# A table of due positions rewritten: stores of V times rms_g, loads, conversions and late attention placed anew in a memory attention and SwiGLU kernel

## The chip, the cores and the metric

The kernel runs on one core of one Trainium2 chip. The metric is the device time of one execution in microseconds (us). Its engines are TensorE (PE, with its weight loads shown apart as PEld), VectorE (DVE), ScalarE (ACT), GpSimd (POOL) and SyncE (SP); in this kernel SP issues every DMA, in the order of its own list. Each engine works through its list strictly in order and waits where an operand isn't there yet.

## The reference

```python
# q, k, v: (8 batches, 8 heads, 576, 64); phi: (8, 8, 576, 32); all float32
a = phi - max(phi, over the 32); a = exp(a); a = a / (sum(a) + 1e-9)
k_m = einsum('bhsm,bhsd->bhmd', a, k)          # sums over all 576 positions
v_m = einsum('bhsm,bhsd->bhmd', a, v)
scores = q @ k_m.T / sqrt(64)
attn = softmax(scores over the 32 memories)
x = (attn @ v_m), heads side by side           # 4608 tokens x 512
# then a gated network on x, with one rms_g for each of the 512 columns
xn = x / sqrt(mean(x * x) + 1e-6) * rms_g
out = (silu(xn @ w_gate) * (xn @ w_val)) @ w_out   # 512 -> 1536 -> 512, float32
```

`setup_inputs` multiplies q and k by 200, so the scores are large and the result has to be computed in full float32 accuracy.

## The kernel before, in words

**Numbers.** Every product of the gated network is made of three: each operand is split into a high and a low part (`ath`/`atl`, `xh`/`xl`, `wh`/`wl`, `oh`/`ol`, `hh`/`hl`) and high-high, high-low and low-high are added up in PSUM. The network is not applied to x itself: V times rms_g (`vg`) is multiplied into the weights first (`vp`, `vq`), so that the attention weights meet a 64-wide product `xh`/`xl` of V and W, and 1/rms is computed from a Gram matrix (`gram`) of V and the attention weights, and multiplied into these weights (L236).

**Part 1 (0 to about 150 us).** The eight batches go through one after the other, and two of them are a pair. For a batch: `load_phi` and eight loads of k and v into buffers `kv` (each is free again when the product matmuls of the batch that used it have ended); the softmax of phi, for which DVE takes maxima (`mc`, L549), PE turns them (`mt` L556, `mr` L573), DVE subtracts (L582) and ACT takes the exponential into `e_bd` (L592); 72 matmuls `kvp` (L623) that make k_m and v_m in one PSUM tile; 64x1 matmuls with ones (L638) that add the denominators into the same tile, from `e_bd` directly or from partial sums `es` that POOL has made; then on DVE `si` (L646, L647), `im` (L649), `kb` and `vb` (L655); the transposes `kvt` on PE (L667), their copies on ACT (L681), `vg` on POOL (L688), and the Gram products (L697, L706). For batches 4 to 7 `store()` (L713, and L716 for `gram`) writes `vg` and, for the second batch of a pair, the Gram matrix to DRAM; the first sweep reads both back.

The attention of pairs 0 and 1 is done here too: for each of four steps q is loaded and turned, 36 matmuls make the scores S (L763), DVE takes maxima and subtracts them (`mxs` L774, L776), ACT takes the exponential, the sums `sm` are made (by one DVE reduction, L790; or by a POOL addition that halves the row and a DVE reduction, L796; or by five POOL additions), POOL multiplies by 1/`sm` (L803, tile `a`). Then `x_steps`: PE turns `a` (`tp`, L208), DVE or ACT copies it into `at` (L218), PE multiplies by the Gram matrix (`xp`, L265/270), DVE squares and adds (L283), a chain of short DVE steps makes 1/rms (`rinv`, L294 to L311), PE spreads it (`rp`, L228), DVE multiplies it into `at` (L236), and ACT and POOL split `at` (L256, L257).

Beside this the first weights are converted: `raw` is loaded, DVE makes a rounded copy in integer arithmetic (`ex`, `mi`, L387 to L417), a multiplication (`w`, L433) on POOL or DVE closes it, and the split parts are stored to `wd`, `od` (L457, L462) for the second sweep.

**Sweeps.** The first sweep (about 150 to 560 us) takes pairs 0 and 1 against twelve blocks of weights, in 24 units: `vp` (L964), `pg` and `pv` (L1000), the gate (L1008, L1009), the split (L1027, L1028), `po` (L1047), `acc` (L1055), and the output (L1059). Spread among them are the conversion of the other weights and the late attention of pairs 2 and 3. The second sweep (units 24 to 47) takes pairs 2 and 3; for it the weight parts are reloaded from DRAM (`reload`, L475), `vq` (L914) multiplies V into them, and `send` (L945) moves the result to its place.

**What sets the order.** One dictionary, `PRM`, gives a due position to every step. The program collects pairs of position and function, sorts them by position and calls them; the lists of the engines come out of that order, after a scheduler of the framework has arranged it by its own estimate of times, which it does again for each program. So a position is a wish, and the order of the lists has to be read from the program built. Those that this text names are `K_AT` and `POST` (products and DVE steps of a batch), `PREP`, `PD` (softmax of phi), `KD` (loads of k and v), `SO`, `X_AT` (attention of pairs 0 and 1), `VD` (the stores of `vg`), `CV` (conversion), `U` and `RL` (units of the second sweep and their reloads). `XE`, `SUM`, `CE` and `ESN` don't place a step: they choose the engine of a copy L218, the way of a sum, the engine of a multiplication L433, and how many of a batch's partial sums POOL adds up ahead of L638. Of this are the lines

```python
ev.append((K_AT[b] + 6 * PRM["KP"] + PRM["POST"][5] + PRM["VD"][b - 2 * G], store))
on_pool = kind == 2 or n >= 2 or PRM["CE"][n] & (1 << kind)
for _, f in sorted(ev, key=lambda e: e[0]):
    f()
```

## Time and profile before

| what | value |
|---|---|
| median of 3 runs | 895.3 us (894.73 to 896.17) |
| profiled execution, its own time | 894.66 us |
| its span | 892.9 us, so 1.76 us lie around the span |
| TensorE clock granted, mean | 0.971 |
| PE busy | 829.4 us (93%), 5919 matmuls |
| DVE, ACT, POOL busy | 543.8, 400.7 and 326.7 us |
| DMA | 131.62 MB, 147 GB/s on average |

All durations that follow come from this one profiled execution; its time is 0.64 us under the median. In the rows, L numbers are lines of the kernel before, an arrow points from the operand to the result, and an expression in brackets at a row's end tells how long the engine had waited ahead of the instruction and for whom. "x36" at the end of a row of the timeline is the number of like instructions that the row stands for.

### The profile page before, as it was taken

Reading aid. Unit: us, or ns where it says so; the run is one execution under the profiler, and the core shown is the slowest. Engines: PE = TensorE matmul, PEld = TensorE weight load, DVE = VectorE, ACT = ScalarE, POOL = GpSimd, SP = SyncE. Lnnn points to the kernel's source line nnn. Section 1 sums busy time; section 2 is a strip of 40 time slices with the busy share of each in tenths; the row PEclk is TensorE's granted clock in tenths of the full one; section 3 lists DMA queues with packets and bytes.
Section 4 is the critical chain, followed back from the end, with each engine's and each line's share of the span. In section 5 each row is a group of like instructions: output and inputs, shape, how many; then the busy total and the mean of one; then the engine's idle time right before and its main releaser. Section 6 shows DMA issues by size and latency. Waiting matters only on the chain.

```text
span 892.9 us, 15977 instructions
## 1 busy us (share of the span) xinstructions
PE 829.4 (93%) x5919; PEld 738.3 (83%) x5919; DVE 543.8 (61%) x982; ACT 400.7 (45%) x715; POOL 326.7 (37%) x272
## 2 busy tenths in 40 slices
PE   4889576999999999998999999999999999999997
PEld 4777466989897988987997988878989898999996
DVE  5587965888757887877987746412344344444434
ACT  1666442676854664645654433335423223233220
POOL 3464744465435454354363531412212112122120
PEclk9889787999999999999999999999999999999999
DMA  8987542545335254253353455575655555553437
GB/s 277 323 276 241 204 145 85 150 145 158 108 98 143 77 146 118 78 182 118 91 145 115 147 129 114 139 216 136 171 139 130 135 144 144 140 149 87 92 93 170
DMA packets 110245, 131.62 MB, mean 147 GB/s; under 512 B 45140, under 2 KB 74840, under 8 KB 110168
## 3 DMA queue, kind: packets, MB, share of 16 engines
q1 hardware_dynamic: 110168, 130.60, 51.5%
q8 instruction: 47, 0.77, 0.4%
q14 instruction: 30, 0.25, 0.1%
HBM read 73.93 MB, written 31.46 MB: 118 GB/s over the span
## 4 chain that ended last, share of the span: by engine, by line
PE 66%; DVE 14%; DMA 6%; issue 5%; ACT 4%; POOL 4%; SPq 2%; DVEq 0%; POOLq 0%; ACTq 0%
PE po L1047 26%; PE pg L1000 13%; PE pv L1000 12%; PE kvp L623 4%; PE vp L964 3%; PE vq L914 2%; DVE xl L977 2%; POOL w L433 1%; DVE ex L387 1%; POOL hl L1028 1%; DMA oh<-od 1%; SPq L945 1%; DVE acc L1055 1%; DMA kv<-in_v_dram 1%; DVE mi L417 1%
## 5 line engine op out<-in xcount | busy, mean ns | idle before, releaser
L1028 POOL TENSOR_TENSOR hl<-hf,hh 128x512 fp32r<-128x512 f32 (+1 forms) x86 | 126.6, 1474 | 271.4 <-ACT hh L1027 247.5
L1055 DVE TENSOR_TENSOR acc<-po,acc 128x512 f32<-128x512 f32 x180 | 123.4, 687 | 138.4 <-PE po L1047 137.4
L1047 PE MATMUL po<-oh,hh 128*128 128x512 f32 x387 | 154.6, 401 | 6.4 <-DMA oh<-od 2.9
L1047 PE MATMUL po<-ol,hh 128*128 128x512 f32 x387 | 153.0, 395 | 0.2 <-DMA xl<-sl 0.2
L1047 PE MATMUL po<-oh,hl 128*128 128x512 f32 x387 | 152.9, 395 | 0.0
L1009 DVE TENSOR_TENSOR hf<-pv,sg 128x256 f32<-128x256 f32 x192 | 85.4, 452 | 89.3 <-PE pv L1000 46.2
L1008 ACT ACTIVATE sg<-pg 128x256 f32<-128x256 f32 x192 | 77.0, 409 | 132.3 <-PE pg L1000 124.6
L1000 PE MATMUL pg<-ath,xh 128*128 128x320 f32 (+1 forms) x384 | 86.4, 300 | 5.7 <-ACT xh L976 3.4
L1047 PEld LDWEIGHTS po<-oh,hh 128*128 128x128 f32 x387 | 72.6, 188 | 19.5 <-DVE acc L1055 4.5
L1000 PE MATMUL pv<-ath,xh 128*128 128x320 f32 (+1 forms) x384 | 86.4, 298 | 0.7 <-DVE hf L1009 0.7
L1047 PEld LDWEIGHTS po<-oh,hl 128*128 128x128 f32 x387 | 72.7, 188 | 17.0
L1000 PE MATMUL pg<-ath,xl 128*128 128x320 f32 (+1 forms) x384 | 85.4, 295 | 0.0
L1000 PE MATMUL pv<-atl,xh 128*128 128x320 f32 (+1 forms) x384 | 85.4, 297 | 0.0
L1000 PE MATMUL pv<-ath,xl 128*128 128x320 f32 (+1 forms) x384 | 84.7, 295 | 0.0
L1000 PE MATMUL pg<-atl,xh 128*128 128x320 f32 (+1 forms) x384 | 84.0, 296 | 0.0
L1047 PEld LDWEIGHTS po<-ol,hh 128*128 128x128 f32 x387 | 72.8, 188 | 9.7 <-DMA ol<-od 1.1
L433 POOL TENSOR_TENSOR w<-mi,ex 128x512 f32<-128x512 f32 x34 | 43.8, 1288 | 90.9 <-ACT mi L424 48.7
L1027 ACT CAST hh<-hf 128x512 fp32r<-128x512 f32 (+1 forms) x86 | 57.7, 673 | 41.6 <-DVE hf L1009 35.9
L1000 PEld LDWEIGHTS pg<-ath,xh 128*128 128x128 f32 x384 | 63.9, 189 | 11.2 <-ACT xh L976 3.7
L977 DVE TENSOR_TENSOR xl<-vp,xh 64x1024 fp32r<-64x1024 f32 x48 | 58.5, 1220 | 16.0 <-ACT xh L976 15.0
L1000 PEld LDWEIGHTS pv<-ath,xh 128*128 128x128 f32 x384 | 64.2, 190 | 4.3 <-PE qtp L1109 0.9
L1000 PEld LDWEIGHTS pg<-ath,xl 128*128 128x128 f32 x384 | 63.9, 188 | 1.9
(145 smaller groups left out, 1549.5 us busy)
## 6 DMA issues: line engine op xcount, KB each, us to landing
xh<-sh SPq DMA_DIRECT2D x192, 64.0 KB, 2.1
xl<-sl SPq DMA_DIRECT2D x192, 64.0 KB, 2.0
kv<-in_k_dram SPq DMA_DIRECT2D x32, 288.0 KB, 5.5
kv<-in_v_dram SPq DMA_DIRECT2D x32, 288.0 KB, 5.9
out_dram<-acc SPq DMA_DIRECT2D x72, 128.0 KB, 2.4
raw<-in_moe_w_gate_dram SPq DMA_DIRECT2D x12, 512.0 KB, 4.5
raw<-in_moe_w_val_dram SPq DMA_DIRECT2D x12, 512.0 KB, 4.1
wd<-wh SPq DMA_DIRECT2D x24, 256.0 KB, 3.4
```

Source lines behind the costliest of these rows:

```text
L433: (nc.gpsimd if on_pool else V).tensor_tensor(out=d["w"], in0=m, in1=ex, op=ALU.mult)
L623: nc.tensor.matmul(kvp[64 * par:64 * par + 64, cc, 0:128], e_bd[j][:, hp, c, :], st["kv", b, hp][:, :, 64 * c:64 * c + 64], start=(c == 0) ...
L914: nc.tensor.matmul(vp[:, h, e, :], vall[a][:, cc, k:k + 4, :].rearrange("p q m -> p (q m)"), w, start=(a == 0), stop=(a == 1),)
L964: nc.tensor.matmul(vp[:, cc, e, :], lhs(l), r[:, 2 * cc + e, :], start=(n == 0), stop=(n == 2),)
L977: urgent.append(nc.vector.tensor_tensor(out=xl[rows], in0=src, in1=xh[rows].bitcast(F32), op=ALU.subtract).ins)
L1000: nc.tensor.matmul(pt[:, :N], l[cc][:, b, half * P:half * P + P], r[:, cc, b, t0:t0 + n, :].rearrange("p t x -> p (t x)"), start=(m == 0), ...
L1008: nc.scalar.activation(sg[:, :N], pg[:, :N], AF.Silu)
L1009: urgent.append(nc.vector.tensor_tensor(out=hf[:, :, b, :], in0=pv[:, :N].rearrange("p (t x) -> p t x", x=64), in1=sg[:, :N].rearrange("p ...
L1027: nc.scalar.copy(hh, hv)
L1028: nc.gpsimd.tensor_tensor(out=hl, in0=hv, in1=hh.bitcast(F32), op=ALU.subtract)
L1047: nc.tensor.matmul(po, l[:, tt, :], r, start=(m == 0), stop=(m == 5))
L1055: nc.vector.tensor_tensor(out=accs[key], in0=po, in1=accs[key], op=ALU.add).ins
```

## The change

Only the table `PRM` changes; the functions stay as they are. Since the new table is one line shorter, each line of the program behind it has a number lower by one (L655 of before is L654 of the changed kernel). Nearly all positions move a little; `K_AT`, `PREP`, `POST`, `VD`, `U`, `RL` and the late attention's `AO`, `XM`, `LV` move most. Of the choices of engine, `CE`, `XE`, `ESN` and `SUM` differ. The diff, cut to those that the text speaks of:

```diff
-    K_AT=[12.08, 15.05, 41.68, 67.52, 100.72, 122.69, 147.6, 167.28],
-    POST=[-0.15, 3.05, 3.9, 7.72, 15.27, 21.96],
-    PREP=[-1.56, 0.79, 2.32, 3.9, 18.7],
-    PD=[2.1, 11.67, 7.79, 18.42, 7.54, 2.17],
+    K_AT=[13.363, 15.05, 40.4, 67.638, 100.72, 121.436, 147.375, 167.28],
+    POST=[-0.321, 0.971, 3.924, 6.647, 13.774, 23.564],
+    PREP=[1.51, 4.063, 4.804, 6.408, 19.983],
+    PD=[2.916, 10.458, 5.724, 18.42, 6.66, 0.895],
...
-    SO=[3.76, 13.53, 20.6, 28.62],
-    X_AT=[102.5, 152.9],
+    SO=[6.301, 15.134, 17.877, 25.896],
+    X_AT=[99.973, 151.3],
...
-    CE=[2, 1],
-    XE=[28, 29, 14, 13],
-    ESN=[3, 3, 2, 3, 3, 3, 2, 3],
-    SUM=[1, 0, 1, 0, 2, 1, 2, 1],
+    CE=[2, 3],
+    XE=[12, 25, 29, 21],
+    ESN=[2, 3, 2, 3, 3, 3, 2, 1],
+    SUM=[0, 0, 1, 0, 0, 1, 2, 1],
...
-    LV=[21.0, 21.1, 22.22, 22.25],
-    VD=[0.01, 0.01, 0.01, 0.01],
+    LV=[20.212, 20.066, 20.345, 21.465],
+    VD=[21.975, 26.245, 17.499, 12.102],
...
-    RL=[-2.85, -3.4, -3.3],
-    RW=[1.73, 1.6],
+    RL=[-1.958, -3.528, -4.083],
+    RW=[1.928, 1.302],
```

So beside the order, five things differ. The sums of steps 0 and 4 of pairs 0 and 1 (`SUM`) are each made by one DVE reduction; before, step 0 had one POOL addition and a DVE reduction, and step 4 five POOL additions. The multiplication L433 of weight 1 of w_val (`CE`) goes from DVE to POOL. Two of the copies L218 go from ACT to DVE (`XE`; tp8 of pair 0, tp4 of pair 1). Batch 0 has one POOL addition less and batch 7 two less (`ESN`), and instead 8 and 16 more of the 64x1 matmuls L638. Nothing else is added or removed; SP issues the same 774 DMAs.

The first of three places is VectorE around 104 to 114 us, where 1/rms of pair 0 ends (`rinv`), batch 5 gives `kb` and `vb`, and batch 7's softmax of phi begins (`mc`). Before:

```order
L311 SCALAR_TENSOR_TENSOR rinv_70<-u_1178,rinv_70 128x9
L774 TENSOR_REDUCE mxs_3_1366<-S_3_1270 128x18
L776 TENSOR_TENSOR ex_3_1368<-S_3_1270,mxs_3_1366 128x576
L236 TENSOR_TENSOR at_900<-at_900,rp_0_1253 128x1024
L646 TENSOR_SCALAR si_1310<-kvp_1197 128x2
L236 TENSOR_TENSOR at_900<-at_900,rp_4_1319 128x1024
...
L796 TENSOR_REDUCE sm_3_1469<-half_3_1470 128x18
L549 TENSOR_REDUCE mc_0_1350<-phi_1344 128x128
...
L649 TENSOR_TENSOR im_1313<-si_1310,hmask 128x4
L801 TENSOR_SCALAR sm_3_1469<-sm_3_1469 128x18
L655 TENSOR_TENSOR kb_1315<-kvp_1197,im_1313 128x256
L655 TENSOR_TENSOR vb_1316<-kvp_1197,im_1313 128x256
```

In the changed kernel:

```order
L645 TENSOR_SCALAR si_1296<-kvp_1201 128x2
L310 SCALAR_TENSOR_TENSOR rinv_70<-u_1169,rinv_70 128x9
L646 RECIPROCAL si_1296<-si_1296 128x2
L648 TENSOR_TENSOR im_1299<-si_1296,hmask 128x4
L654 TENSOR_TENSOR kb_1301<-kvp_1201,im_1299 128x256
L654 TENSOR_TENSOR vb_1302<-kvp_1201,im_1299 128x256
L235 TENSOR_TENSOR at_882<-at_882,rp_0_1238 128x1024
L235 TENSOR_TENSOR at_882<-at_882,rp_4_1259 128x1024
L773 TENSOR_REDUCE mxs_3_1378<-S_3_1310 128x18
...
L548 TENSOR_REDUCE mc_0_1363<-phi_1353 128x128
L775 TENSOR_TENSOR ex_3_1380<-S_3_1310,mxs_3_1378 128x576
```

The steps of batch 5 now stand right behind the last step of 1/rms; before, the score steps of pair 1 (L774, L776), two multiplications L236 and a maximum L549 stood ahead of them. These now come behind.

The second place is SP around 105 to 124 us, where the first store of `vg` (batch 5, `vgd_75`) stands; `kv` are loads of batches 6 and 7, and the last `raw` is weight 1 of w_val. Before:

```order
L462 DMA wd_82<-wl_1361 64x1024 x2
L713 DMA vgd_75<-vg_1356 128x256
L333 DMA kv_3_1447<-in_k_dram 128x576
L716 DMA gd_66<-gram_1301 128x256
L333 DMA kv_3_1447<-in_v_dram 128x576
L333 DMA kv_1_1559<-in_k_dram 128x576
L333 DMA kv_1_1559<-in_v_dram 128x576
L333 DMA kv_2_1601<-in_k_dram 128x576
L333 DMA kv_2_1601<-in_v_dram 128x576
L333 DMA raw_1681<-in_moe_w_val_dram 128x4x256
```

In the changed kernel:

```order
L461 DMA wd_82<-wl_1350 64x1024 x2
L332 DMA kv_3_1429<-in_k_dram 128x576
L332 DMA kv_3_1429<-in_v_dram 128x576
L332 DMA kv_1_1553<-in_k_dram 128x576
L332 DMA kv_1_1553<-in_v_dram 128x576
L712 DMA vgd_75<-vg_1359 128x256
L715 DMA gd_66<-gram_1334 128x256
L332 DMA kv_2_1606<-in_k_dram 128x576
L332 DMA kv_2_1606<-in_v_dram 128x576
L332 DMA raw_1618<-in_moe_w_val_dram 128x4x256
```

The store moved behind the four loads of `kv_3` and `kv_1`; the loads of `kv_2` and of `raw` are still behind it. The stores of batches 4, 6 and 7 keep their places but for a neighbour or two.

The third place is SP at the start of the second sweep (545 to 590 us), where outputs of the first sweep (`acc`) and the reloads of weights 14 (`wd_84`), 15 (`wd_85`) and of w_out (`od`) stand. Before:

```order
L1059 DMA out_dram<-acc_3_2614 64x512 x2
L475 DMA wh_6413<-wd_84 128x1024
L475 DMA wl_6414<-wd_84 128x1024
L1059 DMA out_dram<-acc_4_2673 64x512 x2
...
L1059 DMA out_dram<-acc_8_2776 64x512 x2
L475 DMA oh_6572<-od_94 128x512
L475 DMA ol_6573<-od_94 128x512
L475 DMA oh_6576<-od_95 128x512
L475 DMA ol_6577<-od_95 128x512
L475 DMA wh_6720<-wd_85 128x1024
L475 DMA wl_6721<-wd_85 128x1024
```

In the changed kernel:

```order
L1058 DMA out_dram<-acc_6_2415 64x512 x2
L474 DMA wh_6294<-wd_84 128x1024
L474 DMA wl_6295<-wd_84 128x1024
L944 DMA xh_6298<-sh_0_6170 32x512
...
L1058 DMA out_dram<-acc_8_2791 64x512 x2
L474 DMA wh_6601<-wd_85 128x1024
L474 DMA wl_6602<-wd_85 128x1024
L474 DMA oh_6605<-od_94 128x512
L474 DMA ol_6606<-od_94 128x512
```

The reload of weight 14 now stands among the outputs of pair 0 (`acc_6` there, an earlier tile of that name), some 35 rows earlier; that of weight 15 moved ahead of the w_out parts.

More of the change, by code (lines that the diff above doesn't have):

```diff
@@ L33 @@
-    QD=[5.05, 6, 3, 5, 23.44, 20.6, 19, 15.8],
-    PD0=0.96,
-    QL=3.73,
-    OL=3.83,
-    QO=[-0.32, 1.73, -1.7, 0.7, 1.27, 3.23],
-    SO=[3.76, 13.53, 20.6, 28.62],
-    X_AT=[102.5, 152.9],
-    XP=1.78,
-    LAG=0.79,
-    CV=114.79,
-    CP=3.53,
-    CV2=155.67,
-    CP2=0.05,
+    K_AT=[13.363, 15.05, 40.4, 67.638, 100.72, 121.436, 147.375, 167.28],
+    KP=0.894,
+    POST=[-0.321, 0.971, 3.924, 6.647, 13.774, 23.564],
+    P1=4.4,
+    PREP=[1.51, 4.063, 4.804, 6.408, 19.983],
+    PD=[2.916, 10.458, 5.724, 18.42, 6.66, 0.895],
@@ new lines @@
+    EXP=[2.881, 16.813, 2.683, 5.571, 14.966, 5.079],
+    ES=1.147,
+    PH=[8.971, 16.192, 42.386, 73.222, 103.794, 132.737],
+    S_AT=[32.67, 47.351, 51.02, 66.609, 103.56, 110.637, 115.802, 122.673],
+    KD=[-15.069, -118.205, -42.204, -7.345, -6.094, -14.765, -0.175, -2.835, -28.265, -16.685, -20.115,
+        -8.311, -12.025, -12.235, -27.337, -18.831, -22.801, -22.01, -23.715, -24.999, -11.785, -13.845,
+        -5.925, -9.825, -16.375, -22.685, -11.543, -19.501, -66.165, -9.755, -3.235, -20.028],
@@ L46 @@
+    QD=[7.304, 6.29, 3, 5.412, 23.44, 19.844, 13.088, 15.8],
+    PD0=1.426,
+    QL=3.658,
+    OL=3.392,
+    QO=[-1.196, 3.962, -1.81, 0.678, -0.019, 2.768],
+    SO=[6.301, 15.134, 17.877, 25.896],
+    X_AT=[99.973, 151.3],
+    XP=1.802,
+    LAG=0.815,
+    CV=111.983,
+    CP=3.361,
+    CV2=155.844,
+    CP2=0.194,
     QE=[0, 0],
-    CE=[2, 1],
-    XE=[28, 29, 14, 13],
-    ESN=[3, 3, 2, 3, 3, 3, 2, 3],
-    SUM=[1, 0, 1, 0, 2, 1, 2, 1],
+    CE=[2, 3],
+    XE=[12, 25, 29, 21],
+    ESN=[2, 3, 2, 3, 3, 3, 2, 1],
@@ L78 @@
-    RW=[1.73, 1.6],
+    RO=2.93,
+    RS=5.558,
+    RP=0.998,
+    GV=[0.154, 0.211, 0.356, 0.672, 0.849, 0.849],
+    VW=[-0.188, -0.138, 0.023],
+    VW0=0.405,
+    O=[0.127, 0.297, 0.451, 0.514, 0.879, 0.974, 1.344, 1.487, 1.518],
+    PRE=[-0.625, 0.045, 0.25, 1.342, 2.044, 2.579],
+    PRE0=[-0.298, 0.749, 1.284, 1.645, 2.36, 2.55],
+    PI=0.136,
+    PSW=[1.981, 2.035, 2.009, 2.679, 3.202, 3.24],
+    SU=[1.874, 3.101, 5.773, 6.557, 9.801, 12.208, 13.357, 15.533],
+    AO=[0.192, 0.207, 0.207, 0.276, 0.382, 0.423, 0.562, 0.581, 0.581, 0.614, 0.614, 0.819, 1.158, 1.378],
@@ L79 @@
+    XB=[17.199, 22.762],
+    XS=[0.1086, 0.0359],
+    XM=[21.908, 25.323],
+    XN=[-0.214, -0.131, 0.013, 0.058, 0.162, 0.514, 0.548, 0.617, 0.617],
+    LV=[20.212, 20.066, 20.345, 21.465],
+    VD=[21.975, 26.245, 17.499, 12.102],
+    U=[[-1.6, -1.6, -1.4, -1.227, -0.99, -0.99], [-1.64, -1.54, -1.172, -1.172, -1.036, -1.03], [-1.6, -1.5,
+        -1.335, -1.152, -0.986, -0.05]],
+    RL=[-1.958, -3.528, -4.083],
+    RW=[1.928, 1.302],
     CB=1,
```

28 lines of the change are left out of this document (removed).

## The prediction

> **What bounds the kernel now.** I read the page's engine totals first, then busy times by stretch, then TensorE's waits, then the timelines around the longest of these.
>
> ```profile
> PE 829.4 (93%) x5919; PEld 738.3 (83%) x5919; DVE 543.8 (61%) x982; ACT 400.7 (45%) x715; POOL 326.7 (37%) x272
> ```
>
> ```profile
> 80.00:120.00 40.00, 27.59 (x364) 22.42 (x366) 38.13 (x78) 19.51 (x38) 25.64 (x30) 0.79 0.45 156
> 120.00:166.00 46.00, 35.38 (x370) 31.95 (x367) 25.00 (x65) 20.49 (x37) 18.38 (x17) 0.81 0.52 153
> ...
> 200.00:240.00 40.00, 39.17 (x253) 35.57 (x252) 31.66 (x47) 30.50 (x54) 20.21 (x15) 1.00 0.48 130
> ...
> 760.00:800.00 40.00, 40.00 (x242) 35.98 (x241) 17.41 (x30) 10.00 (x21) 7.30 (x5) 1.00 0.51 136
> ```
>
> The stretches give the window, its length, the busy time of PE, PEld, DVE, ACT and POOL with their instructions, the granted clock, the DMA share and GB/s. TensorE is without work for 892.9 − 829.4 = 63.5 us. The sweeps have little of that: 0.83 us of 40 in the first, none of 40 in the second. From 80 to 166 us it is 86 − 27.59 − 35.38 = 23.0 us. From 80 to 120 VectorE is busy for 38.13 of 40 us, from 120 to 166 for only 25.00 of 46: there a chain of single waits sets the end, and not any engine's work. Since every matmul stays, a different order can only move waits, and the end of part 1 is where they are. What TensorE waited for up to 166 us (us in all, times, longest):
>
> ```profile
> PE mt L556 <- DVE mc L549: 14.9, 4, 4.9
> PE rp L228 <- DVE rinv L311: 6.2, 2, 4.6
> ```
>
> **The change part by part: 80 to 120 us.** TensorE, and then VectorE, where batch 5 ends and batch 6 begins:
>
> ```profile
> 97.76 1.25 PE L763 MATMUL S<-km,qT 128*64 128x64 f32 x36
> ...
> 104.28 1.08 PE L228 MATMUL rp<-ident,rinv 128*128 128x128 f32 x4 [4.62 <-DVE rinv L311]
> ...
> 111.44 0.45 PE L556 MATMUL mt<-ident,mc 128*128 128x128 f32 x1 [4.52 <-DVE mc L549]
> ...
> 114.19 0.69 PE L667 MATMUL kvt<-ident,kb 128*128 128x128 f32 x2 [2.09 <-DVE kb L655]
> ...
> 115.23 3.64 PE L623 MATMUL kvp<-kv,e_bd 128*64 128x128 f32 x30
> ```
>
> ```profile
> 103.96 0.17 DVE L311 SCALAR_TENSOR_TENSOR rinv<-u,rinv 128x9 f32<-128x9 f32 x1
> ...
> 111.38 2.29 DVE L649 TENSOR_TENSOR im<-si,hmask 128x4 f32<-128x4 f32 x1
> ...
> 113.71 0.42 DVE L655 TENSOR_TENSOR kb<-kvp,im 128x256 f32<-128x256 f32 x1
> ```
>
> ```profile
> L790 DVE TENSOR_REDUCE sm<-ex 128x18 f32<-128x576 f32 x2 | 1.4, 724 | 0.0
> ...
> L218 DVE COPY at<-tp 128x512 f32<-128x512 f32 (+1 forms) x7 | 4.2, 605 | 0.3 <-PE tp L208 0.3
> ```
>
> Between the end of 1/rms (103.96 + 0.17 = 104.13) and `kb` of batch 5 (113.71) VectorE works through 9.6 us of other things, and TensorE waits twice, for `mc` and for `kb`. In the new order those others stand behind `vb`. Ahead of 104.13 come the reduction in place of POOL's additions (0.72) and a copy of half a tile (half of 605 ns, with its fixed part about 0.35): 1/rms ends at 105.2. `im` and `kb` follow at once, done by about 107. TensorE then does `rp` (1.08), the score step that now stands there (1.25), a second `rp` (1.1), so that `kvt` runs at about 108.8 in place of 114.19: 105.3 + 1.08 + 1.25 + 1.1. From `kvt` to the first product of batch 6 the old order takes 115.23 − 114.19 = 1.04, the new one has a last `rp` besides (0.3): batch 6 starts at 110.2, **5.0 us earlier**. `mt` of batch 7, for which PE stood 4.52 us, is now queued behind most of batch 6's products and should wait for nothing. The cover of this gain is TensorE's own work; if `kb` isn't done by 108.8, each us is lost at once, since everything of batch 6 is queued behind `kvt`.
>
> **120 to 150 us.** The next thing late is the load of w_val's second weight. SP stood at the store of `vg` until POOL had made it, and that load, 8 rows behind, was issued at 124.08:
>
> ```profile
> 117.04 0.61 POOL L688 TENSOR_TENSOR vg<-vt,rg 128x256 f32<-128x256 f32 x1
> ```
>
> ```profile
> 117.67 0.33 SPq L713 DMA_DIRECT2D vgd<-vg  x1
> ```
>
> ```profile
> 124.08 6.13 DMA raw<-in_moe_w_val_dram
> ```
>
> The store goes behind two pairs of `kv` loads, which no longer wait for it. The raw load stays behind the last pair, whose buffer comes free when batch 6's products have come far enough: it follows their start by 124.08 − 115.23 = 8.85 us, so it goes out at 119.1 and lands 6.13 later, at 125.2, **5.0 earlier**. VectorE has the passed work to do meanwhile (9.6 us and the rest of its list), and I have it arrive at the conversion just before that.
>
> ```profile
> 130.31 0.43 DVE L387 TENSOR_SCALAR ex<-raw 128x512 int32<-128x512 int32 x1 [3.23 <-DMA raw<-in_moe_w_val_dram]
> ...
> 140.19 0.43 DVE L283 CUSTOM_DVE_ANT_0 xp<-xp,a 128x256 f32<-128x256 f32 x1 [3.41 <-PE kvp L623]
> ...
> 144.32 0.15 DVE L646 TENSOR_SCALAR si<-kvp 128x2 f32<-128x2 f32 x1
> ...
> 147.83 1.55 DVE L433 TENSOR_TENSOR w<-mi,ex 128x512 f32<-128x512 f32 x1
> 149.31 0.41 DVE L236 TENSOR_TENSOR at<-at,rp 128x256 f32<-128x256 f32 x1
> ```
>
> ```profile
> 127.71 0.66 PE L270 MATMUL xp<-gb,at 128*64 128x128 f32 x8
> ...
> 136.03 3.57 PE L623 MATMUL kvp<-kv,e_bd 128*64 128x128 f32 x33
> ...
> 139.92 2.24 PE L623 MATMUL kvp<-kv,e_bd 128*64 128x128 f32 x37
> 141.94 0.37 PE L638 MATMUL kvp<-ones,es 128*64 128x1 f32 x6
> ...
> 142.64 0.26 PE L638 MATMUL kvp<-ones,e_bd 128*64 128x1 f32 x2
> ...
> 149.77 0.58 PE L964 MATMUL vp<-wh,vm 128*128 128x256 f32 x1 [1.37 <-DVE at L236]
> ```
>
> ```profile
> 121.85 1.55 PE kvp L638 x37
> ```
>
> ```profile
> L649 DVE TENSOR_TENSOR im<-si,hmask 128x4 f32<-128x4 f32 x3 | 2.9, 982 | 0.1
> ```
>
> The last square of pair 1 ended at 140.6, after a wait of 3.41 behind batch 7's products. In the new order those stand wholly behind the last `xp`. So the squares end at 140.6 − 3.4 − 5.1 (VectorE's wait, as far as the load is earlier) + 1.4 (the last sum of pair 1 now stands behind `im` and `kb` of batch 6, 0.98 + 0.42 by the rows of their kinds) + 0.6 (a copy moved from ACT) = 134.1. TensorE is free just before, and batch 7's products take 139.92 + 2.24 − 136.03 = 6.1, less 0.7 for the `xp` among them: 5.4: 139.4. The sums took 142.64 + 0.26 − 141.94 = 0.96; 16 more, two records each, at 1.55/37 = 0.042 make 1.3 more: `si` of batch 7 starts at about 141.6, **2.7 earlier** than 144.32, and the 1/rms of pair 1 (144.32 − 140.6 = 3.7 us from 134.1) is hidden by the products. From `si` to the first `vp` it was 149.77 − 144.32 = 5.45, in which the multiplication L433 stood between two of L236 with 149.31 − 147.83 = 1.48 of its 1.55. That goes to POOL: 141.6 + 5.45 − 1.48 = 145.6. The first sweep starts **4.2 us earlier**.
>
> The multiplication on POOL is hidden as long as POOL is done before the second `vp` wants the weight; POOL has 18.38 busy of 46 us there, and the same kind takes 1.29 us on it:
>
> ```profile
> L433 POOL TENSOR_TENSOR w<-mi,ex 128x512 f32<-128x512 f32 x34 | 43.8, 1288 | 90.9 <-ACT mi L424 48.7 <-DVE ex L404 21.8 <-DVE hf L1009 12.5
> ```
>
> ```profile
> 107.51 5.03 POOL L257 TENSOR_TENSOR atl<-at,ath 128x512 fp32r<-128x512 f32 x4
> ```
>
> [...]
>
> Up to 80 us I take 0: eight more matmuls for batch 0 cost at most 16 × 0.042 = 0.7 us, and a POOL addition less ahead of them gives about as much. Bounds: 1 us either way.
>
> **The sweeps.** The first sweep's order changes nearly everywhere. I value that at 0: with 0.83 us idle in 40, the ten such stretches from 166 to 560 us have 8 us to win, and nothing there shows a wait that this order surely removes; bounds are half of that won, 4, and 2 lost. In the second sweep the reloads move.
>
> ```profile
> 587.64 0.74 PE L1047 MATMUL po<-oh,hh 128*128 128x512 f32 x2 [1.04 <-DMA oh<-od]
> ```
>
> ```profile
> 577.21 7.40 SPq L1059 DMA_DIRECT2D out_dram<-acc  x10
> ```
>
> ```profile
> 586.73 7.13 DMA wh<-wd
> ```
>
> ```profile
> wh<-wd SPq DMA_DIRECT2D x12, 512.0 KB, 4.6
> ```
>
> Weight 15 goes out right behind the outputs, 577.21 + 7.40 = 584.6 in place of 586.73, but its `vq` now stands ahead of the first `po` that waited, where TensorE arrives at 587.64 − 1.04 = 586.6. By the median landing (4.6) it waits 584.7 + 4.6 − 586.6 = 2.7, by the slow one seen (7.13) 5.2. The wait that it replaces was 1.04. So: −1.0 if the landing is covered, +1.7 by the median, +4.2 by the slow one. Weight 14 goes out early and its `vq` stands early as well; I take 0 for it. In all +0.3, the middle of the first two: the new list has other `po` work ahead of that `vq`, but how long it lasts I can't read.
>
> **Sum.** 894.66 − 4.2 + 0.3 = 890.8 for a profiled execution. The median is 0.64 above that execution, so I say **891.4 us**.
>
> **The rivals.** *More than that* (R1): the first sweep's gaps close too. For it: conversions and late attention, which feed TensorE there, are all placed anew, and 8 us of gaps are there. Against: no single wait there is long. Half of the gaps, 4.1, gives 887.3.
>
> *Given back* (R2): the 5.0 us of batch 6 don't reach the sweep. The raw load is still behind the store of `vg`, and `vg` is made by a POOL that is busy for 25.64 of 40 us; if it isn't earlier, the conversion still starts at about 130.3, behind it the squares, and the passed VectorE work of 9.6 us fills what was idle. Only the multiplication is left, 1.48, less the 1.3 of added sums: −0.2 + 0.3, so 895.4, no change. The 3.23 us of idle time ahead of that load speak for it, the earlier `kvt` against.
>
> *Slower* (R3): the reloads land late. If they need the 7.13 seen at 586.73 in place of 4.6, `vq` of weight 15 costs 4.2 net, and that of weight 14, 2.5 us more than the median would (7.13 − 4.6). With 4.2 won this is +2.5: 897.8. For a landing of L us the two cost L − 2.9 and L − 4.6, so that it decides, past the 4.2 won and the 1.8 that can be told, from L = 6.8 us on. For it: the slow landing is in the trace at that very place, right behind outputs and reloads of w_out. Against: the median of the twelve is 4.6.
>
> That the change doesn't do what its words say is partly so already: of four stores of `vg` only one moves behind loads, and this is in the sum.
>
> **How the numbers follow.** The forecast has 0.46, R1 0.20, R2 0.18, R3 0.16. What a measurement of this kernel can tell from no change is about 0.2%, 1.8 us: faster is below 893.5, slower above 897.1. Forecast and R1 are faster (0.66), R2 is the same (0.18), R3 slower (0.16). The forecast's own range, by the bounds of sweep and early part, is 888 to 894; the full range goes 2.3 below R1's time, since its gaps may close by more than half, and up to R3's: 885 to 897.5.
>
> **What would show it.** Right: batch 6's products start near 110, with no wait for `kb` over 0.5 us; the conversion behind the raw load starts near 125; the first `vp` near 145.6; TensorE's idle time up to 166 us is some 4 us less, and that of the second sweep within 2 us of before. R2 shows as a first `vp` near 149.5, R3 as waits for `wh` or `wl` over 3 us at `vq` between 545 and 600 us, R1 as a first sweep shorter by 3 us from `vp` to 560. Wrong: a first `vp` later than 149.77 at all, or a sweep longer by over 3 us without a wait for a reload; then the price of order in the sweep, which I set to 0, is the fault.

## The result and the profile after

The changed kernel takes 885.0 us (median of 6 runs, 882.68 to 889.06) where the kernel before takes 895.37 (median of 6, 893.44 to 897.51): a ratio of 0.989 with a 95% interval of 0.986 to 0.992. That is 10.4 us less, where 3.9 was forecast. Measured again beside other kernels it had 888.4 against 897.1, ratio 0.9905 (0.9876 to 0.9934), 8.7 us less. The profiled execution of the first measurement took 886.18 us, its span 884.4.

The page's engine totals and the busy times by stretch, of the changed kernel:

```profile
PE 833.2 (94%) x5967; PEld 744.0 (84%) x5967; DVE 545.3 (62%) x983; ACT 398.5 (45%) x714; POOL 319.9 (36%) x264
```

```profile
80.00:120.00 40.00, 31.01 (x438) 26.15 (x437) 35.74 (x81) 20.30 (x40) 22.70 (x24) 0.88 0.60 197
120.00:166.00 46.00, 38.87 (x370) 34.84 (x370) 26.73 (x72) 22.64 (x41) 19.48 (x18) 0.81 0.44 119
...
200.00:240.00 40.00, 40.00 (x261) 36.73 (x260) 30.10 (x46) 30.31 (x53) 17.96 (x15) 1.00 0.50 139
```

TensorE is busy 3.8 us more (48 records more, the 24 added small matmuls) and has 884.4 − 833.2 = 51.2 us without work in place of 63.5. From 80 to 166 us it is 86 − 31.01 − 38.87 = 16.1 in place of 23.0, and the stretch 200 to 240, in the first sweep, has none where it had 0.83.

The place around `kvt` of batch 5, on TensorE and on VectorE:

```profile
104.60 1.11 PE L227 MATMUL rp<-ident,rinv 128*128 128x128 f32 x4 [2.20 <-DVE kb L654]
...
109.02 0.69 PE L666 MATMUL kvt<-ident,kb 128*128 128x128 f32 x2
...
110.26 2.07 PE L622 MATMUL kvp<-kv,e_bd 128*64 128x128 f32 x33
...
113.91 0.33 PE L555 MATMUL mt<-ident,mc 128*128 128x128 f32 x1
```

```profile
103.97 0.16 DVE L648 TENSOR_TENSOR im<-si,hmask 128x4 f32<-128x4 f32 x1
104.16 0.42 DVE L654 TENSOR_TENSOR kb<-kvp,im 128x256 f32<-128x256 f32 x1
...
123.80 0.43 DVE L386 TENSOR_SCALAR ex<-raw 128x512 int32<-128x512 int32 x1 [2.61 <-DMA raw<-in_moe_w_val_dram]
...
140.22 0.16 DVE L645 TENSOR_SCALAR si<-kvp 128x2 f32<-128x2 f32 x1 [3.46 <-PE kvp L637]
```

`kb` is made at 104.16 where it was 113.71, `kvt` runs at 109.02 without a wait, `mt` of batch 7 waits for nothing, and batch 6's products start at 110.26 in place of 115.23. Their first 33 records took 2.07 us where 30 had taken 3.64: TensorE also ran them faster, which the section on the hardware comes back to. One wait is put down to `kb`, the 2.20 ahead of `rp`: TensorE starts that `rp` as `kb` ends, 0.74 us behind the end of 1/rms (103.86), where before it started 0.15 behind; so at most 0.6 of the wait belongs to `kb`, the rest to 1/rms. The end of part 1:

```profile
133.45 4.15 PE L622 MATMUL kvp<-kv,e_bd 128*64 128x128 f32 x72
...
144.45 0.58 PE L963 MATMUL vp<-wh,vm 128*128 128x256 f32 x1 [0.31 <-DVE at L235]
```

The first `vp` is at 144.45, 5.3 us earlier. All of TensorE's work behind it, up to the end of its last matmul, lasted 738.5 us before (149.77 to 888.25) and 735.2 now (144.45 to 879.70). TensorE's gaps behind the first `vp` sum to 15.7 us in place of 20.9. These are one execution of each kernel; the experiments show how far single executions differ.

### The profile page after: what moved, and what is told of

It is laid out like the page before. It is cut to its first block, busy times and chain, and to the rows that moved or that the text cites. A ratio compares the mean times of both kernels' runs of the same rounds, so it can differ in the third digit from the quotient of the medians.

```text
span 884.4 us, 16052 instructions
## 1 busy us (share of the span) xinstructions
PE 833.2 (94%) x5967; PEld 744.0 (84%) x5967; DVE 545.3 (62%) x983; ACT 398.5 (45%) x714; POOL 319.9 (36%) x264
## 4 chain that ended last, share of the span: by engine, by line
PE 76%; DVE 9%; DMA 6%; ACT 3%; issue 3%; SPq 2%; POOL 1%; POOLq 0%; DVEq 0%; ACTq 0%
PE po L1046 31%; PE pv L999 15%; PE pg L999 15%; PE vp L963 3%; PE kvp L622 3%; PE vq L913 3%; DMA phi<-in_phi_dram 1%; PE S L1129 1%; PE xp L269 1%; DVE mi L411 1%; PE tp L207 1%; DMA oh<-od 1%; DVE xl L976 1%; DVE mc L548 1%; DVE mi L416 1%
## 5 line engine op out<-in xcount | busy, mean ns | idle before, releaser
L1046 PEld LDWEIGHTS po<-oh,hl 128*128 128x128 f32 x387 | 72.7, 188 | 17.1
L1046 PEld LDWEIGHTS po<-oh,hh 128*128 128x128 f32 x387 | 72.6, 188 | 15.3 <-DVE acc L1054 4.0
L1046 PEld LDWEIGHTS po<-ol,hh 128*128 128x128 f32 x387 | 72.8, 188 | 10.4 <-DMA ol<-od 1.4
L432 POOL TENSOR_TENSOR w<-mi,ex 128x512 f32<-128x512 f32 x35 | 45.2, 1291 | 99.0 <-ACT mi L423 49.0
L999 PEld LDWEIGHTS pv<-ath,xl 128*128 128x128 f32 x384 | 63.7, 190 | 2.2
```

The source lines that it names most:

```text
L432: (nc.gpsimd if on_pool else V).tensor_tensor(out=d["w"], in0=m, in1=ex, op=ALU.mult)
L999: nc.tensor.matmul(pt[:, :N], l[cc][:, b, half * P:half * P + P], r[:, cc, b, t0:t0 + n, :].rearrange("p t x -> p (t x)"), start=(m == 0), ...
L1046: nc.tensor.matmul(po, l[:, tt, :], r, start=(m == 0), stop=(m == 5))
```

## The experiments

Eleven other kernels and the changed one again ran in three groups of four, each group beside its own runs of the kernel before (medians 894.7, 894.4 and 897.1). A median of 6 to 12 runs is uncertain by about 0.3%, nearly 3 us, so smaller differences are read from the traces, and each trace is one execution. The ratios, and four numbers from each trace (when batch 6's products and `si` of batch 7 start, the time from this `si` to the first `vp`, and the time from there to the end of TensorE's work):

| kernel | ratio to before (interval) | batch 6 | si of 7 | si to vp | vp to end |
|---|---|---|---|---|---|
| before | 1 | 115.2 | 144.3 | 5.45 | 738.5 |
| changed | 0.989 (0.986 to 0.992) | 110.3 | 140.2 | 4.23 | 735.2 |
| part 1 new | 0.9965 (0.9941 to 0.9989) | 107.5 | 137.5 | 4.23 | 738.0 |
| sweeps new | 0.9942 (0.9919 to 0.9966) | 114.8 | 143.6 | 4.91 | 733.2 |
| one number | 0.9939 (0.9917 to 0.9960) | 107.7 | 139.6 | 4.91 | 737.1 |
| stores back | 0.991 (0.988 to 0.994) | 109.4 | 139.6 | 4.24 | 738.3 |
| one number, mult. to POOL | 0.994 (0.9915 to 0.9965) | 108.2 | 141.0 | 4.91 | 736.0 |
| sums on POOL | 0.9938 (0.9917 to 0.9960) | 109.1 | 138.5 | 7.05 | 734.6 |
| combined from parts | 0.9934 (0.9911 to 0.9957) | 109.6 | 142.5 | 4.91 | 735.2 |
| reloads back | 0.9932 (0.9906 to 0.9959) | 110.8 | 140.7 | 4.24 | 739.1 |
| changed, again | 0.9905 (0.9876 to 0.9934) | 110.2 | 140.3 | 4.23 | 738.0 |
| sums on POOL, order kept | 0.9879 (0.9848 to 0.9911) | 108.4 | 138.7 | 5.27 | 734.4 |
| reloads alone | 0.9991 (0.9971 to 1.0011) | 113.9 | 142.6 | 4.84 | 739.8 |
| first sweep alone | 0.9913 (0.9884 to 0.9943) | 115.8 | 144.6 | 4.90 | 735.5 |

Single executions differ by more than most of the effects. Five profiles have the changed table's part 1 and one and the same list on VectorE up to the first `vp` (changed twice, part 1 new, stores back, reloads back): batch 6 starts in them between 107.5 and 110.8. In the four with the part 1 of before (before, sweeps new, reloads alone, first sweep alone) it starts between 113.9 and 115.8. The means, 109.6 and 114.9, are 5.3 us apart. From there to the first `vp` the five take 34.3 us on average and the four 33.9: what part 1 wins is won at batch 6, and nothing is added behind it.

### Part 1 and the sweeps apart

The table was split: the part-1 numbers of the changed table with the sweeps' numbers of before, and the other way round.

```diff
 # part 1 new: all of these from the changed table, the sweeps' as before
+    K_AT, KP, POST, P1, PREP, PD, EXP, ES, PH, S_AT, KD, QD, PD0, QL, OL, QO, SO, X_AT, XP, LAG,
+    CV, CP, CV2, CP2, CE, ESN, SUM, RO, RS, RP, VD, XE of pairs 0 and 1
 # sweeps new: all others from the changed table, part 1 as before
+    GV, VW, VW0, O, PRE, PRE0, PI, PSW, SU, AO, XB, XM, XN, LV, U, RL, RW, XE of pairs 2 and 3
```

`XE` has a part in both: for pairs 2 and 3, whose attention is done late, in the first sweep, it gives five copies L218 to another engine (three to ACT, two to DVE), besides the two of pairs 0 and 1.

> The kernel before with all numbers of part 1 from the changed table (and its engine choices there), the sweeps' numbers as before. Theory A (the two stages win separately: 5.3 us up to the first vp, 149.77 to 144.45, and 5.3 us of TensorE's gaps in the sweeps, 20.9 to 15.7): first vp near 144.5, gaps behind it still about 21 us, time 5 us under before, ratio 0.994. Rival C (the sweeps' gaps close only because the first sweep starts earlier): gaps behind the first vp fall to about 16 here too, time 10 us under before, ratio 0.989.

> The other half: the changed table's numbers for the sweeps, part 1 as before. Theory A: first vp near 149.8 as before, TensorE's gaps behind it about 16 us in place of 20.9, time 5 us under before, ratio 0.994. Rival C: gaps near 21, no change, ratio 1.000.

Measured: 891.7 us for part 1 new and 889.8 for the sweeps new, against 894.7. The two gains, 2.9 and 4.9 us, make nearly 8 us together, where the whole change has 10.4 and 8.7. With the new part 1 the work behind the first `vp` lasts 738.0 as before (738.5), and TensorE's gaps there sum to 21.7 us against 20.9; with the new sweeps it lasts 733.2, and the first `vp` stays late, at 148.51. So each stage wins without the other, and rival C, by which the sweeps' numbers alone change nothing, falls. Theory A isn't borne out in full: the gaps with the new sweeps alone are 18.5, midway between its 16 and the rival's 21. That the new part 1 has a share in closing them comes out further below. Theory A's 5 us for part 1 were measured as 2.9 (1.0 to 5.3 by the interval); the profiled execution of that kernel, with a first `vp` at 141.72, was the fastest of its twelve and says more than the median bears out.

### One number of part 1

```diff
 # before, with one number changed
-    X_AT=[102.5, 152.9],
+    X_AT=[99.973, 152.9],
```

In the built order this puts `kb` of batch 5 two places behind the last step of 1/rms, where the whole change has three and the kernel before thirteen. The scheduler also rearranged other instructions, on POOL and SP too, so the cause has to be read from TensorE's waits.

> The kernel before with one number changed, the position of pair 0's x steps (the first of X_AT, 102.5 to 99.973). In the built order this alone puts si, im, kb and vb of batch 5 right behind the last step of 1/rms; the store of vg stands one pair of loads later, the multiplication L433 stays on VectorE. The prediction's step (kb of batch 5 is what batch 6 waits for): batch 6's products start near 110 in place of 115.2, and the first vp comes about 3.5 us earlier (5.3 measured for the whole change, less 1.5 for L433): ratio 0.996. Rival D (the gain in part 1 comes from the many other moves): batch 6 starts within 1 us of 115.2 and the time doesn't change, ratio 1.000.

Measured: 889.2 us against 894.7. On TensorE of that kernel:

```profile
106.75 0.64 PE L667 MATMUL kvt<-ident,kb 128*128 128x128 f32 x2
...
107.74 2.30 PE L623 MATMUL kvp<-kv,e_bd 128*64 128x128 f32 x26
```

Batch 6 starts at 107.74, and the first `vp` comes at 144.46. In place of the waits of before, 4.62 for 1/rms, 4.52 for `mt` and 2.09 for `kb`, TensorE has one of 7.65 ahead of `rp`, where 1/rms ends, and 0.32 for `mt`; `kvt` waits for nothing. Rival D falls: what batch 6 waited for was VectorE's work in the wrong order, `kb` and `mc` behind the rest. Of the 6 us won at batch 6 not all arrives: over the three profiles with this one number (the two others are below) `si` of batch 7 starts at 141.0 on average, against 143.8 over the four with the old part 1, and the first `vp` comes at 145.9 against 148.8. The five profiles with the whole new part 1 (changed twice, part 1 new, stores back, reloads back) have 139.7 and 143.9. So by the traces this one number carries about 3 of the 5 us of part 1 (two of its three profiles also hold a loss of 1 us that is told below). The other 2 are lost between batch 6 and the first `vp`, which take 37.4 us with the one number and 34.3 with the whole new part 1; which of its numbers do that wasn't tested. By the times the one number alone has 5.5 us (3.6 to 7.4), no less than the whole of part 1 with its 2.9 (1.0 to 5.3); the intervals overlap. The expected 3.5 lies at the edge of its interval.

### The stores of vg put back

```diff
 # the changed kernel
-    VD=[21.975, 26.245, 17.499, 12.102],
+    VD=[0.01, 0.01, 0.01, 0.01],
```

> The changed kernel with only the stores of vg (VD) put back. In the built order just two instructions of SP move, nothing on any other engine. If the store of batch 5's vg holds the loads behind it as it did before, the load of w_val's second weight is issued later (124.08 before) and the first vp comes up to 1.6 us later than 144.45: ratio to before 0.991. If, as the prediction has it, that load waits for the last pair of kv loads anyway: no difference to the changed kernel, 0.989.

Measured: 887.9 us, ratio 0.991; the changed kernel had 0.989 and 0.9905. SP's rows, of this kernel and then of the changed one:

```profile
112.64 0.38 SPq L713 DMA_DIRECT2D vgd<-vg  x1
...
117.03 0.38 SPq L333 DMA_DIRECT2D raw<-in_moe_w_val_dram  x1
```

```profile
114.33 0.38 SPq L712 DMA_DIRECT2D vgd<-vg  x1
...
117.53 0.38 SPq L332 DMA_DIRECT2D raw<-in_moe_w_val_dram  x1
```

With the store at its old place the load goes out at 117.03, with the new place at 117.53; `si` to `vp` is the same 4.24. The store no longer holds anything, since batch 5's `vg` is made 5 us earlier. What the change's title names first is worth nothing that these runs can show.

### The multiplication moved to POOL

```diff
 # the kernel with the one number of X_AT
-    CE=[2, 1],
+    CE=[2, 3],
```

> The one number of pair 0's x steps and, besides, the multiplication L433 of w_val's second weight on POOL (CE); all else as before. The prediction's step: 1.48 us off VectorE just ahead of the first vp, so that this comes at about 143.0 where the one number alone had 144.46, and the time is 1.5 us lower, ratio to before 0.992. Rival: something else ends last there by then (1/rms, kvt of batch 7), and the first vp stays within 0.5 us of 144.5. [...]

Measured: 888.5 us against 894.4, ratio 0.994: no better than the one number alone. The first `vp` is at 145.89, not 143.0. The time from `si` of batch 7 to the first `vp` is 4.91 us with the multiplication on VectorE and 4.91 with it on POOL. VectorE at that place, with the multiplication there (one number alone) and without it:

```profile
143.12 0.69 DVE L433 TENSOR_TENSOR w<-mi,ex 128x512 f32<-128x512 f32 x1
143.99 0.42 DVE L236 TENSOR_TENSOR at<-at,rp 128x256 f32<-128x256 f32 x1 [0.19 <-PE rp L228]
```

```profile
139.34 0.17 DVE L311 SCALAR_TENSOR_TENSOR rinv<-u,rinv 128x9 f32<-128x9 f32 x1
139.54 1.12 DVE L309 TENSOR_TENSOR u<-rinv 128x9 f32<-128x9 f32 x1
140.69 0.17 DVE L310 TENSOR_TENSOR u<-u,m 128x9 f32<-128x9 f32 x1
...
145.42 0.42 DVE L236 TENSOR_TENSOR at<-at,rp 128x256 f32<-128x256 f32 x1 [0.79 <-PE rp L228]
```

On VectorE it took 0.69 us and filled a wait for `rp`; without it the same wait is 0.79 long. On POOL it has a price: the row L309, a step of the 1/rms chain that stands ahead of `si`, took 1.12 us where its neighbours take 0.17. POOL of that kernel ran the multiplication just then:

```profile
138.02 1.26 POOL L451 TENSOR_TENSOR wl<-w,wh 128x512 fp32r<-128x512 f32 x1 [7.57 <-DMA gb<-gd]
139.36 1.28 POOL L433 TENSOR_TENSOR w<-mi,ex 128x512 f32<-128x512 f32 x1
```

139.36 + 1.28 = 140.64, and the blocked row ends at 139.54 + 1.12 = 140.66. So the move costs 0.95 us here, of the 1.4 that `si` is later than with the one number alone (140.98 against 139.55); the other 0.5 is there already where batch 6 starts (108.22 against 107.74). `im` of batch 7 took 0.16 (141.37): it was an earlier step that was held.

### The sums back on POOL

```diff
 # the changed kernel
-    ESN=[2, 3, 2, 3, 3, 3, 2, 1],
+    ESN=[3, 3, 2, 3, 3, 3, 2, 3],
```

> The changed kernel with the number of POOL additions for batches 0 and 7 as before (ESN), so 24 fewer 64x1 matmuls (48 records). The prediction's step: they cost 1.3 us ahead of si of batch 7, so that the first vp comes about 1.3 us earlier than 144.45 and the time is 1 us lower, ratio to before 0.988. Rival: the additions are late on POOL and si of batch 7 waits for them; the first vp is no earlier, ratio 0.989 or 0.990.

Measured: 887.8 us against 894.4, ratio 0.9938, no gain over the changed kernel. `si` of batch 7 does start 1.8 us earlier, 138.46 against 140.22, so the additions aren't late on POOL. What the sums take shows directly, from the first to the last of batch 7's matmuls L638: 0.95 us with 24 records in each of the nine traces that have them on POOL, and 2.75 with 56 in each of the five that don't. So the 16 matmuls cost 1.8 us, and not 1.3. But the scheduler then also put two multiplications L236 between `si` and `kb`:

```profile
138.46 0.16 DVE L646 TENSOR_SCALAR si<-kvp 128x2 f32<-128x2 f32 x1 [1.65 <-PE kvp L638]
...
139.04 1.22 DVE L236 TENSOR_TENSOR at<-at,rp 128x1024 f32<-128x1024 f32 x1 [0.22 <-PE rp L228]
140.18 0.83 DVE L649 TENSOR_TENSOR im<-si,hmask 128x4 f32<-128x4 f32 x1
140.93 1.21 DVE L236 TENSOR_TENSOR at<-at,rp 128x1024 f32<-128x1024 f32 x1
142.06 0.41 DVE L655 TENSOR_TENSOR kb<-kvp,im 128x256 f32<-128x256 f32 x1
```

`kb` is at 142.06, and the first `vp` at 145.51, 7.05 behind `si` in place of 4.23. It is the case of batch 5 over again: `kb` behind other work of VectorE, with TensorE waiting. Neither the theory nor the rival had it. So a kernel was made in which VectorE's list is exactly that of the changed kernel (those of TensorE and SP differ in places):

```diff
 # the changed kernel
-    ESN=[2, 3, 2, 3, 3, 3, 2, 1],
-    X_AT=[99.973, 151.3],
+    ESN=[2, 3, 2, 3, 3, 3, 2, 3],
+    X_AT=[99.973, 152.9],
```

> The changed kernel with batch 7's additions back on POOL (16 fewer 64x1 matmuls) and the position of pair 1's x steps as before, which in the built order keeps VectorE's list exactly as in the changed kernel (with the additions alone put back, a multiplication L236 of 1.22 us had come ahead of im and kb of batch 7). If the sums cost what the prediction gave (1.3 us) and that multiplication ate it: si of batch 7 starts near 138.5, as with the additions alone, the first vp comes near 143.0, and the time is 1 us under the changed kernel of this call. Rival: kb of batch 7 isn't what ends last there, the first vp stays at 144 to 145.

Measured: 885.5 us (6 runs, 879.7 to 888.9) where the changed kernel had 888.4 in the same group (884.2 to 890.2); ratios 0.9879 (0.9848 to 0.9911) and 0.9905 (0.9876 to 0.9934). Its ratio is the lowest of all, but the intervals overlap, and that it is faster than the changed kernel isn't shown. In its trace:

```profile
134.62 0.43 DVE L283 CUSTOM_DVE_ANT_0 xp<-xp,a 128x256 f32<-128x256 f32 x1 [2.11 <-PE kvp L623]
...
137.41 1.20 DVE L310 TENSOR_TENSOR u<-u,m 128x9 f32<-128x9 f32 x1
...
138.73 0.15 DVE L646 TENSOR_SCALAR si<-kvp 128x2 f32<-128x2 f32 x1
...
139.12 0.84 DVE L649 TENSOR_TENSOR im<-si,hmask 128x4 f32<-128x4 f32 x1
139.99 0.42 DVE L655 TENSOR_TENSOR kb<-kvp,im 128x256 f32<-128x256 f32 x1
```

`si` starts 1.5 us earlier than in the changed kernel's two profiles (140.22, 140.27), and the first `vp` comes at 144.00, only 0.5 earlier. `im` took 0.84 in place of 0.40, and the last L236 waits 0.52 for `rp`. As a test of the sums it fails: with the old position of pair 1's x steps some of batch 7's products stand ahead of the last `xp` again, the last square waits 2.11 us for them, a step of 1/rms is held (1.20), and `si` starts at the end of 1/rms, while the sums had ended at 137.32. That it is 1.5 us earlier is the earlier start of batch 6 in this execution, 108.42 against 110.26; from there to `si` it takes 30.3 us, in the changed kernel 30.0. So what the sums are worth at the first `vp` isn't shown.

### A kernel combined from the parts

```diff
 # the kernel before; the sweeps' numbers from the changed table, and
+    X_AT=[99.973, 152.9],
+    CE=[2, 3],
```

> A kernel from the parts: part 1 as before but for the one number of pair 0's x steps and the multiplication L433 on POOL, the sweeps by the changed table. By theory A (part 1 and sweeps win separately) it takes the 5.3 us of the one number, the 5.3 us of the sweeps and up to 1.5 us of the multiplication: 883.5, ratio to before 0.987, a little under the changed kernel. If the changed kernel's part 1 has more to it than these two, it is slower than that kernel: 0.991.

Measured: 889.1 us against 894.4, ratio 0.9934. It isn't the 883.5 expected. The nearest kernel of the same group is "one number, mult. to POOL", which differs from it by the sweeps' numbers alone: 888.5, ratio 0.994. So beside this part 1 the sweeps' numbers bring nothing that the times show, where alone they had brought 4.9; with intervals of 0.25% on either side up to 3 us could be hidden, and a full 4.9 hardly. In the traces the combined kernel has 735.2 from the first `vp` on against 736.0, and starts it 1.56 us later (147.45 against 145.89). Of these 1.40 are there at batch 6 (109.62 against 108.22) though VectorE's lists are the same up to there, so they are the difference of two executions. The 1/rms chain was held twice, L310 for 1.22 us and L309 for 1.12, each until a POOL instruction ended (140.87 and 142.22 where POOL's ended at 140.84 and 142.19), but so it was in the kernel without the sweeps' numbers (1.22 and 1.12). In the changed kernel the chain has ended by 136.8, ahead of these two POOL instructions (138.40 and 139.74), and what is held there is `im`, 0.40 in place of 0.16. Why the parts don't add up here stays open.

### The reloads and the first sweep

```diff
 # reloads back: the changed kernel, with U, RL and RW of before
-    RL=[-1.958, -3.528, -4.083],
-    RW=[1.928, 1.302],
+    RL=[-2.85, -3.4, -3.3],
+    RW=[1.73, 1.6],
 # reloads alone: the kernel before, with U, RL and RW of the changed table
 # first sweep alone: the kernel "sweeps new", with U, RL and RW of before
```

> The changed kernel with the units and reloads of the second sweep as before (U, RL, RW). The prediction gave their move a price of +0.3 us. By that it is the same, ratio to before 0.989 or lower, with waits for oh near 1 us each in place of those for wh and wl at vq of weight 15. Rival: the move took the three waits for oh of before (2.9 us together) away; then they are back and the time is 1.5 to 2.5 us higher, ratio 0.991.

> The kernel before with only the numbers of the second sweep's units and reloads changed (U, RL, RW). The prediction's price: +0.3 us, with the bounds -1.0 and +4.2: waits for wh and wl at vq of weight 15 of 2 to 3 us, the wait of 1.04 for oh gone; gaps from 560 us on within 1 us of 4.2, ratio 1.000. Rival (most of the sweeps' 5.3 us is from here, as three waits for oh go): gaps from 560 us on fall by 2 us or more, ratio 0.997.

> The kernel before with only the first sweep's numbers changed (with conversion and late attention there), neither part 1 nor U, RL, RW. If the sweeps' gain is rival R1 of the prediction (the first sweep's gaps close): gaps from the first vp to 560 us fall from 16.7 to about 12.6 and the time by 3 to 4 us, ratio 0.996. If it is from the reloads: gaps stay near 16.7, ratio 1.000.

Measured: reloads back 888.4 us against 894.4 (0.9932); reloads alone 895.2 against 897.1 (0.9991, interval 0.9971 to 1.0011); first sweep alone 888.9 against 897.1 (0.9913). TensorE at `vq` of weight 15 with the reloads alone:

```profile
588.21 0.50 PE L914 MATMUL vq<-wh,va 128*128 128x256 f32 x2 [2.21 <-DMA wh<-wd]
...
589.47 0.50 PE L914 MATMUL vq<-wl,va 128*128 128x256 f32 x2 [0.76 <-DMA wl<-wd]
```

The wait is there, 2.21 + 0.76 = 3.0 us, and the waits for `oh` of before (2.9 us, three times) are gone: gaps from 560 us on are 3.7 us against 4.2. The move of the reloads pays what it takes. The kernel with the reloads back looks otherwise at first: its ratio is what the rival said or more, and the waits for the weight parts of w_out are back:

```profile
PE po L1047 <- DMA ol<-od: 2.3, 1, 2.3
PE po L1047 <- DMA oh<-od: 1.6, 4, 0.7
```

But its interval (0.9906 to 0.9959) meets those of the changed kernel, and its gaps from 560 us on are 4.1 us against 3.1 and 2.6 there. Over all fourteen traces these gaps are 3.5 us on average in the six kernels with the old reloads and 3.1 in the eight with the new, so the move is worth 0.4 us, and with the reloads alone the rival's 2.7 us doesn't show in the times either. That leaves the first sweep. With its numbers alone the times are 8.2 us (5.1 to 10.4) lower, with the sweeps new 4.9 (3.0 to 7.2). In the trace of the first sweep alone the gaps from the first `vp` to 560 us are 15.1 us against 16.7, not the 12.6 expected, and the work behind the first `vp` lasts 735.5 against 738.5; the profiled execution was the slowest of its six. TensorE's waits from 150 to 560 us, first of the kernel before, then with the first sweep alone:

```profile
PE po L1047 <- DVE acc L1055: 2.1, 5, 0.9
PE pg L1000 <- ACT sg L1008: 1.7, 2, 1.0
PE qtp L1109 <- DVE acc L1055: 1.6, 2, 1.2
PE S L1130 <- ACT qT L1115: 1.4, 2, 1.1
...
PE vp L964 <- DVE xl L977: 1.2, 2, 0.7
```

```profile
PE pv L1000 <- DVE hf L1009: 3.3, 3, 1.7
PE pg L1000 <- ACT sg L1008: 1.0, 1, 1.0
PE vp L964 <- POOL wl L451: 0.7, 2, 0.5
...
PE po L1047 <- DVE acc L1055: 0.6, 1, 0.6
```

Such waits belong to the order: in kernels that share it most of them come back to within some tenths. So the fourteen traces can be put together. The table has the means in us, from the first `vp` to 560 us, and in the last two columns from the first `vp` to the end of TensorE's work; in brackets stands the number of traces, and `acc` at `qtp` is the wait of `qtp` for `acc`:

| kernels | all gaps | `acc` at `qtp` and `po` | `xl` at `vp` | `sg` at `pg` | `hf` at `pv` | `xh` at `pg` | at half clock | vp to end |
|---|---|---|---|---|---|---|---|---|
| old first sweep (5) | 17.1 | 3.9 | 1.0 | 2.2 | 0.7 | 3.6 | 7.4 | 737.9 |
| new, part 1 as before or one number (3) | 15.4 | 0.7 | 0 | 1.0 | 3.3 | 3.6 | 5.7 | 734.6 |
| new, new part 1 (6) | 13.2 | 1.6 | 0 | 1.2 | 0.6 | 5.0 | 15.3 | 736.6 |

The new order takes away the waits for `acc`, `xl` and `sg`; the one for `acc` at `qtp`, 1.6 us in each of the five old ones, is in none of the nine new ones. Alone it brings a new wait for `hf`, 2.7 us more, and that one goes with the new part 1. So the gaps fall by 1.7 us alone and by 3.9 in the changed kernel, and none of the waits that go was long. TensorE also ran at half clock for longer behind the first `vp` in the kernels with both. By an estimate that 1 us at half clock does half its work (a product of batch 6 takes 0.121 us there and 0.063 at full clock), (15.3 − 7.4) / 2 = 4 us of TensorE's time go there, about what the gaps win, and the work behind the first `vp` is only 1.3 us shorter. That the first sweep's numbers make the kernel faster is shown by the times of two kernels, and which waits they close by the traces. How many us of the whole change are theirs isn't shown, since the times say 5 to 8, the combined kernel nothing, and the traces 1 to 3.

### The changed kernel again

> The changed kernel once more, for a second profile and more times beside the next three. By the first: ratio 0.989, first vp near 144.45, TensorE's gaps behind it 15.7 us; a stretch at half clock near 376 to 383 us if that belongs to this order of work (all three profiles with this order of the first sweep have had it), none if it is chance. If the times of the first measurement were lucky: ratio 0.992.

Measured: 0.9905, between the two figures. The first `vp` is at 144.50 (144.45 the first time), gaps behind it 16.5 us (15.7), and the stretch at half clock near 376 us is there again.

## Why the prediction was right, and where it was not

The direction and the mechanism of part 1 were right, and the forecast of 891.4 was too high by 6.4 us against the first measurement. R1, at 887.3, came nearer, and that the full range held 885.0, at its lower end, is luck. Step by step, predicted and then in the profile:

| step | predicted | changed kernel |
|---|---|---|
| `kvt` of batch 5 | 108.8 | 109.02 |
| first product of batch 6 | 110.2 | 110.26 |
| raw load issued | 119.1 | 117.53 |
| conversion behind it | 125.2 | 123.80 |
| batch 7's products | 134.0 | 133.45 |
| `si` of batch 7 | 141.6 | 140.22 |
| first `vp` | 145.6 | 144.45 |

That these come within 1.6 us is luck in part, since the same lists started batch 6 between 107.5 and 110.8 in five executions. Two errors also cancel ahead of `kvt`: 1/rms ended at 103.86 in place of 105.2, and TensorE then took 4.4 us for `rp` and the scores in place of 3.4. The copy of half a tile, estimated at 0.35, took 0.41 (a whole one 0.68).

- **`kb` of batch 5 behind VectorE's other work.** Right, and shown by the one number that moves it. The wait of 4.52 for `mt` is gone as well.
- **The store of `vg`.** Right that the raw load would come about 5 us earlier (6.6 measured), and that its place behind the store doesn't matter; putting the store back shows it. The 8.85 us that I let the load follow batch 6's start were 7.3, because batch 6's products ran faster (0.063 us each in place of 0.121).
- **The extra sums of batch 7, +1.3 us.** Too small: 1.8. Batch 7's products ahead of them took 4.0 us up to the first sum in place of 5.4, which hid it in the table.
- **The multiplication L433, −1.48 us.** The term was mis-sized: it is 0 in a pair of kernels that differ in it alone (4.91 and 4.91 from `si` to `vp`). The 1.55 us of the row were a chance of that one execution, in which a POOL instruction had begun just ahead; in the three other profiles with the same list, and with the one number, the multiplication takes 0.69 and `si` to `vp` 4.84 to 4.91. The changed kernel has 4.23, where TensorE's last `rp` stands ahead of the `vg` products, which I hadn't counted; what the move is worth in that order wasn't tested. The sum took the multiplication on POOL as hidden; there it cost about 0.25 (`im` 0.40 in place of 0.16). (The `im` of 2.29 us of before ran beside the end of L257, 112.54, and then beside L803, with which it ended: 113.67 and 113.65.)
- **The first sweep, 0.** This is the step that failed. The prediction set the new order there to 0 since it removes no single long wait, and gave R1, by which the gaps close, 0.20. In the traces the gaps close by 3.9 us, R1's 4.1 almost to the number, by many small waits that go. The bound was too narrow too: the 8 us of gaps from 166 to 560 us were ten times those of one stretch, and the ten stretches together have 13.3. How much of the time is from this stays open: by the times of the two kernels 5 to 8 us, by the traces less, since more of the sweep ran at half clock (15.3 us on average in place of 7.4).
- **The reloads, +0.3 us.** Right: 0.9991 for the reloads alone, no change within its interval, with a wait of 3.0 us at `vq` of weight 15 (2.0 in the changed kernel) where 2.7 had been worked out from the median landing, and the waits for `oh` gone. R3, the slower rival, needed landings of 6.8 us; weight 15's two parts landed 4.9 and 5.6 us after their issue in the changed kernel.
- **R2, given back.** Didn't happen: the conversion starts 6.5 us earlier.

## What to carry to other kernels

Where an engine is full for a stretch, look for the short instruction on which another engine's whole queue hangs, and follow it in the list: nine other instructions stood ahead of a 0.42 us one, and moving it won 5 to 6 us at the place and about 3 at the end. A move of work between VectorE and GpSimd should be priced by what runs beside it on the other engine and not by one row's duration, which may hold a block (L433 on VectorE took 1.55 us in one trace and 0.69 in another). A new order of many small waits shouldn't be priced at 0 when a bound says 4: put the estimate between the bounds. And where two profiles of the same list differ by 3 us, compare lengths inside a trace, such as the sums' 0.95 and 2.75, or means over several traces, before a difference of 1 us is put down to an edit.
